# Attention, gated MLP and Fourier mixer in one kernel: MLP steps run closer behind the attention units, and weight conversion is tied to the exponentials

## The chip, the cores and the metric

One core of a Trainium2 chip runs the whole program in one launch. The metric is the device time in microseconds, the median of three runs.

## The reference

Three layers follow each other on four batches. Windowed attention with global tokens (32 global and 512 local tokens, 8 heads of 64) gives x of 544 x 512 a batch. A gated MLP takes h = max(x w_in, 0) with 1024 features, a three-tap convolution along the tokens, and returns (h * sigmoid(conv(h))) w_out. The mixer takes two Fourier transforms and keeps the real part, adds it, normalises over the features, and adds max(un w_ch1, 0) w_ch2 with 2048 hidden features:

```
a = softmax(scale * q k^T, window 32, global keys);  x = a v
h = max(x @ w_in, 0);  x = (h * sigmoid(conv3(h))) @ w_out
u = x + real(fft(fft(x, axis=1), axis=2))
out = u + max(norm(u) @ w_ch1, 0) @ w_ch2
```

The weights arrive as 64-bit numbers, which the kernel itself turns into 32-bit ones.

## The kernel before

**Order.** TensorE (PE) and the DMA queue of SyncE (SP) execute in the order in which the program is written. On ScalarE (ACT), VectorE (DVE) and GpSimd (POOL) a planner at build time chooses the order from the data dependences, its own estimate of the times and the priorities that the helpers carry; on the chip each of these engines then runs its list strictly in order. Every tile is guarded by semaphores.

**First stage: units.** A loop over i = 0 to 33 handles attention unit i (a half batch of one pair of heads; 32 of them, and two more rounds to drain). In unit i PE computes the scores of unit i (`s_mm`), the value products of unit i-2 (`pv_mm`), and the transposes of unit i-1 (`t_mm`). DVE adds the mask and finds the maxima (`s_max`, L311), ACT takes the four exponentials (`s_exp`, L323; the last one is kept in `last_exp`), POOL normalises (L334). Every second unit `pv_evac` copies two units' results into x, the high part by ACT (L389) and the rest by DVE (L390). For the global tokens `sg_piece` computes scores in units 8b+5 and 8b+7 with the banks s and t, emptied by DVE (L405); one unit later `pg_trans` transposes them, and two units later, in 8b+7 and 8b+9, `pg_pv` multiplies by v and has its bank copied into x by ACT (L449) and DVE (L450).

**MLP steps.** Between these, unit i runs two MLP steps, u = 2i-LU and u+1, of 64 (16 a batch: 8 feature blocks on the second half of the tokens, then 8 on the first half). Step u has `m_g1` (12 matmuls x by w_in into bank g1, emptied by ACT, L479), `m_conv` (ACT L489, DVE L490 and L491), `m_tanh` (ACT L497), `m_gate` (DVE L508, ACT L509, DVE L510), and three steps later `m_g2` (two halves of 6 matmuls g by w_out into banks a0 to a3). The steps that don't fit into the loop, from `ulast`+1 to 66, run after it. Up to unit SOLO-1 no `m_g2` runs, and attention may use the banks a0 to a3 and g1 as well.

**Weights.** Sixteen MLP weights are converted in units 0 to 8 (`make_w`): ACT (L167), POOL (L168), DVE or ACT for the tail (L172 or L170), DVE (L174, L175), then the split, ACT (L203) and DVE (L204). That block stands in `tc.issue_after(last_exp[0].ins)`: what it puts on ACT stands behind the last exponential of the unit in ACT's list. Twelve mixer weights go through the same conversion ahead of time: `keep_load` fetches the raw tile two units early (into r0 or r1), `keep_make` converts it (without that tie), `keep_store` writes it to DRAM as `kept`. `keep_at` gives them to units KEEP0, KEEP0+2, and so on.

**SP's list** in unit i is: `keep_load` for the tile of unit i+2, `load_qk(i+2)` (its buffer is free after `s_mm`, or `sg_piece`, of unit i-1), in odd units `load_v` (its buffer is free after `pv_mm`, in some after `pg_pv`), `keep_store` for the tile of unit i.

**After the loop** each remaining step takes two or three pieces of the Fourier transform (`fstep`; 49 pieces, of which the mixer's first nine steps take two each), with the banks s and t in turn. `ln` is the normalisation, `fetch_c(k)` loads kept or raw mixer weights. The mixer's 80 steps follow.

Of the kernel before, what the change touches and what calls it, by code (L numbers as in the profile page):

```python
# [26 lines left out]
KC = 608  # L27
NEG = -1.0e30
NF = 274
LU = 13  # L30
TOK = ((0, 290, 0, 292, 1, 1), (290, 254, 288, 256, 37, 39))
SOLO = 8
LAG_G2 = 3
KEEP0 = 10
KEPT = [0, 16, 1, 17, 2, 18, 3, 19, 4, 5, 6, 7]
TAIL = [x for m in range(8, 16) for x in (m, 16 + m)]
NT = 436
# [91 lines left out]
def fused_kernel(ctx: ExitStack, tc: tile.TileContext, d, out):  # L129
# [7 lines left out]
    def prio(c):  # L137
        def deco(f):
            def g(*a, **k):
                with pri(c):  # L140
                    return f(*a, **k)
            return g
        return deco
# [15 lines left out]
    def f32(ap):  # L159
        return ap.bitcast(F32)  # L160
# [40 lines left out]
    def put(pool, tag, val):  # L201
        t = pool.tile([128, 2, 512], F32R, tag=tag, name="w_" + tag)
        act.copy(t[:, 0], val)  # L203
        dve.tensor_sub(t[:, 1], val, f32(t[:, 0]))  # L204
        return t
# [12 lines left out]
    def bank(tag):  # L218
        return ps.tile([128, 512], F32, tag=tag, name="ps_" + tag)
# [25 lines left out]

    keep_at = {KEEP0 + 2 * k: x for k, x in enumerate(KEPT)}

    def keep_tile(i, lag):
        return keep_at.get(i - lag)
# [6 lines left out]
    @prio("keep")  # L256
    def keep_make(x):
        if x is not None:
            packed[x] = put(rb, "o", unpack(mp, w_raw.pop(x), gp, True))
# [22 lines left out]
    smalls, s_bank, last_exp = {}, {}, [None]  # L282
# [152 lines left out]
    @prio("glo")  # L435
    def pg_pv(g, tag):
        b, gg = divmod(g, 2)
        p, v = pg_t.pop(g), v_t[4 * b + 2 + gg]
        o = bank(tag)[:, 0:2 * SG].rearrange("p (c q) -> p c q", c=2)
        for c in range(2):  # L440
            for t in range(5):
                r = slice(0, 96 if t == 4 else 128)
                for h in range(2):
                    n = 2 * c + h
                    mm(o[64 * h:64 * h + 64, c], v[r, t, 64 * n:64 * n + 64], p[r, t, SG * n:SG * n + SG], t == 0, t == 4)
        xh, xl = get_xt(b)
        cs = slice(2 * gg, 2 * gg + 2)
        with pri("ev"):
            act.copy(xh[:, cs, 0:SG], o)  # L449
            dve.tensor_sub(xl[:, cs, 0:SG], o, f32(xh[:, cs, 0:SG]))  # L450
# [15 lines left out]
    @prio("mg1")  # L466
    def m_g1(u, tag):
        if not 0 <= u < NM:
            return
        b, half, m = u // 16, 1 - (u // 8) % 2, u % 8  # L470
        xh, xl = xt_t[b]
        _, _, t0, n, h0, _ = TOK[half]
        o = bank(tag)[:, 0:n]
        w = w_in[m]
        for c in range(4):
            f = slice(128 * c, 128 * c + 128)
            mm3(o, w[:, 0, f], w[:, 1, f], xh[:, c, t0:t0 + n], xl[:, c, t0:t0 + n], c == 0, c == 3)
        with pri("ev"):
            act.activation(hbuf[u % NHB][:, h0:h0 + n], o, AF.Relu, scale=0.5)  # L479
# [14 lines left out]
    @prio("me")  # L494
    def m_tanh(u):
        if 0 <= u < NM:
            act.activation(g_t[u], g_t[u], AF.Tanh, scale=0.5)  # L497
# [45 lines left out]
    with tc.manual_schedule(engines={mybir.EngineType.SP, mybir.EngineType.PE}):  # L543
        load_qk(0)
        sp.dma_start(mask[:, 2:4], d["mask"][:, 2:4])
        load_qk(1)
        sp.dma_start(ident, d["ident"])
        load_qk(2)
        for t in pbuf:
            dve.memset(t[:, :, 224:256], 0.0)  # L550
        for t in sg4s:
            dve.memset(t[:, KC:640], 0.0)
        for t in hbuf:
            dve.memset(t[:, 0:1], 0.0)
            dve.memset(t[:, 293:294], 0.0)
        dve.memset(f32(ones), 1.0 / 512.0)
        dve.memset(eps, 1e-6)

        NU = B * H
        glob = {8 * b + 5 + 2 * k: 2 * b + k for b in range(B) for k in range(2)}  # L560
        wq = [0] + [x for m in range(7) for x in (m + 1, 8 + m)] + [15]
        wsteps = [0, 1, 2, 4, 6, 8, 10, 12, 14, 16]
        fetched = 0
        craw = ap1.tile([128, 24, 2], I32, name="craw")
        cmag = ap1.tile([128, 24], F32, name="cmag")
        for i in range(NU + 2):
            r = i % 8
            live = i < NU
            early = i < SOLO
            us = [2 * i - LU, 2 * i - LU + 1]  # L570
            if live:
                first = s_mm(i, ("s", "t") if not early or i % 2 == 0 else ("a0", "a1"))
                if i == 0:
                    fetch_w(wq[0], first)
                    load_v(0)
                    sp.dma_start(mask[:, 0:2], d["mask"][:, 0:2])
                    fetched = 1
                while fetched < min(16, (2, 4, 7, 10, 13, 16)[min(i, 5)]):
                    fetch_w(wq[fetched])
                    fetched += 1  # L580
                if i == 1:
                    sp.dma_start(craw.rearrange("p a b -> p (a b)"), bits(d["conv_w"]))
                    gp.dma_start(gmask, d["gmask"])
                s_max(i)
            m_tanh(us[0] - 1)
            if 0 <= i - 2 < NU:
                pv_mm(i - 2, "pv" if not early or (i - 2) // 2 % 2 == 0 else "g1")
                if i % 2:
                    pv_evac((i - 2) // 2)
            if live:  # L590
                s_exp(i)
            m_g1(us[0], "g1")
            m_gate(us[0] - 1)
            m_conv(us[0])
            if live:
                s_norm(i)
            if 0 <= i - 1 < NU:
                t_mm(i - 1, ("s", "t") if not early or i % 2 == 0 else ("a2", "a3"))
                t_evac(i - 1)
            m_g2(us[0] - LAG_G2, 0)  # L600
            m_g2(us[0] - LAG_G2, 1)
            m_tanh(us[1] - 1)
            m_g1(us[1], "g1")
            if i > 5 and r in (6, 0):
                pg_trans(glob[i - 1], "s", "t")
            if i > 6 and r in (7, 1):
                pg_pv(glob[i - 2], "pv" if not early else "a3")
            if live and r in (5, 7):
                sg_piece(glob[i], 0, "s")
                sg_piece(glob[i], 1, "t")  # L610
                pg_soft(glob[i])
            m_gate(us[1] - 1)
            m_conv(us[1])
            m_g2(us[1] - LAG_G2, 0)
            m_g2(us[1] - LAG_G2, 1)
            keep_load(keep_tile(i, -2))
            if live and i > 0:
                load_qk(i + 2)
            if live and i % 2:
                load_v((i + 1) // 2)  # L620
            keep_make(keep_tile(i, 0))
            keep_store(keep_tile(i, 0))
            if i == 3:
                from_f64(craw, cmag)
                dve.tensor_scalar(convw2.rearrange("p a b -> p (a b)"), cmag, 2.0, None, op0=ALU.mult)
            if i < 9:
                with tc.issue_after(last_exp[0].ins):
                    for k in range(wsteps[i], wsteps[i + 1]):
                        make_w(wq[k])
        ulast = 2 * (NU + 1) - LU + 1  # L630
        right.close()
# [103 lines left out]
    @prio("cv")  # L735
    def fetch_c(i):
        pool, tag = c_slot(i)
        if i not in kept:
            w_raw[i] = fetch(pool, tag, c_src(i))
            return  # L740
        t = pool.tile([128, 2, 512], F32R, tag=tag, name="w_" + tag)
        sp.dma_start(f32(t), kept[i])
        (ch2 if i > 15 else ch1)[i % 16] = t
# [128 lines left out]
    def fstep(n=1):  # L872
        for _ in range(n):
            step(fq, "fft")
            for c, b in ((1, 1), (0, 2)):
                if b in u_d and c not in uc_t:
                    load_uc(c)
            if 0 in u_d and not lnq and not ln_t:
                lnq.append(ln(0))
                step(lnq)  # L880

    early = 7

    for u in range(ulast + 1, NM + LAG_G2):
        fstep()
        m_tanh(u - 1)
        m_g1(u, "g1")
        m_gate(u - 1)
        m_conv(u)
        if lnq and early:  # L890
            early -= 1
            step(lnq)
        fstep()
        m_g2(u - LAG_G2, 0)
        if u % 2 or u == ulast + 4:
            fstep()
        m_g2(u - LAG_G2, 1)
        if lnq and early:
            early -= 1
            step(lnq)  # L900
        k = u - (NM - 8)
        if 0 <= k < 8:
            fetch_c(k)
        if 0 <= k - 3 < 8:
            fetch_c(16 + k - 3)
    left.close()
# [74 lines left out]
```

## Time and profile before

| | us |
|---|---|
| median of three runs | 811.71 (811.49 to 812.03) |
| profiled execution, its own time | 815.52 |
| its span, first to last instruction | 813.7 |
| TensorE busy in it | 773.2 (95%) |
| VectorE, ScalarE, GpSimd busy | 480.0, 363.7, 156.1 |

The runs shown are 3.81 below the profiled execution. An engine's busy share is an average over stages with different limits, so the stages are read one by one below.

### The profile page before, as it was taken

How to read it: one execution, taken by the hardware profiler on the slowest of the kernel's cores; microseconds unless marked ns; L12 is line 12 of the kernel's file. 1: busy time of each engine (PE TensorE's matmuls, PEld its weight loads, DVE VectorE, ACT ScalarE, POOL GpSimd, SP SyncE). 2: the span in 40 equal slices, each digit the busy share in tenths (PEclk: the TensorE clock that was granted, in tenths of full speed). 3: DMA queues.
4: the chain of work that ended last, by engine and by line, in shares of the span. 5: the costliest groups of instructions: out<-in, count | busy, mean ns of one | idle time of the engine just before them, and what ended most of it. 6: DMA issues, size and time to landing. Idle time of an engine off the chain costs nothing.

```text
span 813.7 us, 13611 instructions
## 1 busy us (share of the span) xinstructions
PE 773.2 (95%) x5272; PEld 708.3 (87%) x5272; DVE 480.0 (59%) x1167; ACT 363.7 (45%) x884; POOL 156.1 (19%) x213
## 2 busy tenths in 40 slices
PE   6589999899999999999999999999999999999997
PEld 4378888798889888899988999998999999999997
DVE  6999886668676877679794587734421232223113
ACT  6788776567666666545344175412113112211110
POOL 5644521222222132000033012100013002200000
PEclk9779999899999999999999999999999999999999
DMA  8903603333333341226621290011020020001001
GB/s 314 389 34 106 213 28 124 131 132 108 124 129 117 128 131 54 61 78 236 202 104 49 76 379 16 1 41 48 23 67 1 1 88 1 1 1 44 1 1 44
DMA packets 36944, 77.80 MB, mean 96 GB/s; under 512 B 3768, under 2 KB 22072, under 8 KB 36880
## 3 DMA queue, kind: packets, MB, share of 16 engines
q1 hardware_dynamic: 36288, 74.52, 26.5%
q0 software_dynamic: 592, 2.42, 1.2%
q8 instruction: 41, 0.67, 0.3%
q14 instruction: 23, 0.19, 0.1%
HBM read 61.72 MB, written 15.20 MB: 95 GB/s over the span
## 4 chain that ended last, share of the span: by engine, by line
PE 74%; DVE 10%; DMA 9%; ACT 4%; SPq 1%; issue 1%; POOL 1%; DVEq 0%; POOLq 0%; ACTq 0%
PE ps_a L146 30%; PE ps_g L146 19%; PE ps_pv L146 14%; DMA raw_r<-in_ch_dram 7%; PE ps_s L146 5%; PE ps_t L146 4%; DVE mag L174 1%; DMA craw<-in_conv_w_dram 1%; DVE w_w L204 1%; DVE mag L175 1%; DMA uc<-u_d 1%; ACT mag L167 1%; DVE pb L311 1%; SPq L280 1%; ACT raw_r L170 1%
## 5 line engine op out<-in xcount | busy, mean ns | idle before, releaser
L146 PE MATMUL ps_g<-x,w_w 128*128 128x256 f32 (+1 forms) x768 | 113.0, 297 | 4.9 <-ACT h L479 4.9
L146 PE MATMUL ps_a<-g,w_w 128*128 128x254 f32 (+1 forms) x768 | 113.7, 297 | 0.2 <-DVE u L541 0.2
L146 PEld LDWEIGHTS ps_g<-x,w_w 128*128 128x128 f32 x768 | 102.0, 192 | 11.0 <-ACT h L479 6.0
L146 PEld LDWEIGHTS ps_a<-g,w_w 128*128 128x128 f32 x768 | 102.0, 192 | 4.5 <-issue 3.8
L334 POOL TENSOR_SCALAR pb<-pb,sm 128x224 f32<-128x224 f32 x128 | 75.6, 606 | 156.5 <-DVE sm L329 70.2
L146 PE MATMUL ps_a<-hd,w_w 128*128 128x436 f32 (+1 forms) x480 | 101.4, 360 | 0.0
L146 PEld LDWEIGHTS ps_a<-hd,w_w 128*128 128x128 f32 x480 | 90.1, 188 | 4.8
L825 DVE SCALAR_TENSOR_TENSOR hd<-ps_g,hd 128x436 fp32r<-128x436 f32 (+1 forms) x40 | 24.3, 608 | 89.2 <-ACT hd L824 89.2
L146 PE MATMUL ps_a<-hd,w_v 128*128 128x436 f32 (+1 forms) x360 | 76.2, 360 | 0.0
L825 DVE SCALAR_TENSOR_TENSOR hd<-ps_pv,hd 128x436 fp32r<-128x436 f32 (+1 forms) x40 | 24.2, 606 | 85.1 <-ACT hd L824 85.1
L824 ACT ACTIVATE hd<-ps_pv 128x436 fp32r<-128x436 f32 (+1 forms) x40 | 21.3, 532 | 114.9 <-PE ps_pv L146 114.9
L146 PEld LDWEIGHTS ps_a<-hd,w_v 128*128 128x128 f32 x360 | 67.6, 188 | 3.7
L824 ACT ACTIVATE hd<-ps_g 128x436 fp32r<-128x436 f32 (+1 forms) x40 | 21.3, 533 | 110.7 <-PE ps_g L146 110.4
L168 POOL TENSOR_SCALAR mag<-mag 128x512 f32<-128x512 f32 x48 | 36.8, 769 | 161.9 <-ACT mag L167 160.8
L323 ACT ACTIVATE pb<-pb,sm 128x224 f32<-128x224 f32 x128 | 60.4, 474 | 14.4 <-DVE sm L311 14.1
L490 DVE SCALAR_TENSOR_TENSOR y<-h,convw,y 128x254 f32<-128x254 f32 (+1 forms) x64 | 34.1, 533 | 33.9 <-ACT y L489 33.4
L146 PE MATMUL ps_g<-chl,w_w 128*128 128x436 f32 (+1 forms) x240 | 51.0, 361 | 0.0
L146 PE MATMUL ps_pv<-chl,w_v 128*128 128x436 f32 (+1 forms) x240 | 50.8, 360 | 0.0
L146 PE MATMUL ps_pv<-chl,w_w 128*128 128x436 f32 (+1 forms) x240 | 50.8, 360 | 0.0
L146 PE MATMUL ps_s<-qk 64*128 64x224 f32 (+1 forms) x144 | 38.6, 418 | 11.7 <-DMA qk<-in_qk_dram 6.9
L146 PEld LDWEIGHTS ps_pv<-chl,w_v 128*128 128x128 f32 x240 | 45.0, 188 | 2.5
L146 PEld LDWEIGHTS ps_g<-chl,w_w 128*128 128x128 f32 x240 | 44.8, 188 | 2.7 <-issue 0.3
(221 smaller groups left out, 1427.6 us busy)
## 6 DMA issues: line engine op xcount, KB each, us to landing
v<-in_v_dram SPq DMA_DIRECT2D x16, 640.0 KB, 4.4
qk<-in_qk_dram SPq DMA_DIRECT2D x16, 464.0 KB, 6.9
raw_r<-in_ch_dram SPq DMA_DIRECT2D x14, 512.0 KB, 6.3
raw_v<-in_ch_dram SPq DMA_DIRECT2D x13, 512.0 KB, 9.7
kept<-w_o SPq DMA_DIRECT2D x12, 512.0 KB, 7.7
w_w<-kept SPq DMA_DIRECT2D x12, 512.0 KB, 4.2
qk<-in_qk_dram SPq DMA_DIRECT2D x16, 304.0 KB, 6.4
u_d<-u SPq DMA_DIRECT2D x4, 1088.0 KB, 5.2
```

The lines of the kernel that those rows point to most:

```text
L146: return pe.matmul(o, a, b, start=start, stop=stop)
L167: act.activation(mag, f32(head), AF.Abs, scale=65536.0)
L168: (clamp or dve).tensor_scalar(mag, mag, TOP, 2.0, op0=ALU.min, op1=ALU.max)
L170: act.activation(tail, tail.bitcast(U32), AF.Copy, scale=0.999 * 2.0**-29, bias=-0.499)
L174: dve.scalar_tensor_tensor(val, val, 3, tail, op0=ALU.logical_shift_left, op1=ALU.bitwise_or)
L175: dve.scalar_tensor_tensor(val, head, -(2**31), val, op0=ALU.bitwise_and, op1=ALU.bitwise_or)
L204: dve.tensor_sub(t[:, 1], val, f32(t[:, 0]))
L323: last_exp[0] = act.activation(p, p, AF.Exp, bias=sm[:, k:k + 1], scale=-1.0, accum_out=sm[:, 4 + k:5 + k])
L334: gp.tensor_scalar(p, p, sm[:, k:k + 1], 1.0, op0=ALU.mult, op1=ALU.mult)
L490: dve.scalar_tensor_tensor(y, hb[:, cc - 1:cc - 1 + n], convw2[:, m, 0:1], y, op0=ALU.mult, op1=ALU.add)
L824: act.activation(hd[:, 0], o, AF.Relu)
L825: dve.scalar_tensor_tensor(hd[:, 1], o, 0.0, f32(hd[:, 0]), op0=ALU.max, op1=ALU.subtract)
```

## The change

`LU` goes from 13 to 11, so each unit runs MLP steps that are two further on, and two fewer steps are left behind the loop (10 instead of 12). `SOLO` goes from 8 to 7 with it, because the first `m_g2` now comes in unit 7. `KEEP0` goes from 10 to 11: the kept tiles go to odd units. `pg_pv` moves ahead of the unit's second `m_g1`, and always uses bank pv. `keep_make` is put behind the unit's last exponential on ACT. After the loop each step takes three pieces of the transform, and since the first such step is now 57, `fetch_c(0)` comes together with `fetch_c(1)`.

```diff
-LU = 13
+LU = 11
-SOLO = 8
+SOLO = 7
-KEEP0 = 10
+KEEP0 = 11
             m_tanh(us[1] - 1)
+            if i > 6 and r in (7, 1):
+                pg_pv(glob[i - 2], "pv")
             m_g1(us[1], "g1")
             if i > 5 and r in (6, 0):
                 pg_trans(glob[i - 1], "s", "t")
-            if i > 6 and r in (7, 1):
-                pg_pv(glob[i - 2], "pv" if not early else "a3")
...
-            keep_make(keep_tile(i, 0))
+            with tc.issue_after(last_exp[0].ins):
+                keep_make(keep_tile(i, 0))
             keep_store(keep_tile(i, 0))
...
         m_g2(u - LAG_G2, 0)
-        if u % 2 or u == ulast + 4:
-            fstep()
+        fstep()
         m_g2(u - LAG_G2, 1)
...
-        if 0 <= k < 8:
-            fetch_c(k)
+        for x in (0, 1) if k == 1 else (k,):
+            if 0 <= x < 8:
+                fetch_c(x)
```

## Rows read from the trace of the kernel before

**Rows 1.** The page: PE's busy time (parts 1 and 2).

```profile
PE 773.2 (95%) x5272; PEld 708.3 (87%) x5272; DVE 480.0 (59%) x1167; ACT 363.7 (45%) x884; POOL 156.1 (19%) x213
...
PEclk9779999899999999999999999999999999999999
```

**Rows 2.** Stages: length, then busy us of PE, PEld, DVE, ACT, POOL, clock, DMA.

```profile
29.86:83.15 53.29, 45.01 (x400) 36.72 (x399) 50.55 (x141) 42.56 (x111) 26.59 (x34) 0.88 0.37 131
...
120.00:337.30 217.30, 206.61 (x1901) 186.06 (x1899) 151.68 (x471) 139.71 (x396) 49.07 (x91) 0.98 0.34 110
337.30:405.70 68.40, 66.33 (x495) 61.70 (x492) 55.05 (x118) 32.43 (x74) 1.82 (x4) 1.00 0.51 164
```

**Rows 3.** PE's waits from 120 to 337.3: total us, times, longest.

```profile
PE ps_g L146 <- ACT h L479: 4.5, 3, 2.8
PE ps_t L429 <- ACT pt L353: 3.2, 3, 1.3
PE ps_s L344 <- DVE sm L311: 3.0, 2, 1.5
```

**Rows 4.** ACT's waits from 80 to 337: total us, times, longest.

```profile
ACT mag L167 <- DMA raw_r<-in_ch_dram: 18.8, 11, 3.0
```

**Rows 5.** The chain that ended last, at unit 14: start, us, what.

```profile
123.71 7.39 DMA raw_r<-in_ch_dram
...
131.13 0.68 ACT mag L167
```

**Rows 6.** Timeline: ACT's first exponential of unit 16 (start, us).

```profile
150.19 0.48 ACT L323 ACTIVATE pb<-pb,sm 128x224 f32<-128x224 f32 x1 [0.99 <-DVE sm L311]
```

**Rows 7.** Timeline: PE in unit 16, behind its longest wait.

```profile
156.29 2.93 PE L146 MATMUL ps_g<-x,w_w 128*128 128x256 f32 x12 [2.82 <-ACT h L479]
...
159.93 2.70 PE L146 MATMUL ps_a<-g,w_w 128*128 128x254 f32 x12
```

**Rows 8.** The stretch around it, columns as in rows 2.

```profile
155.40:162.30 6.90, 6.01 (x28) 6.02 (x29) 3.38 (x8) 3.85 (x11) 0.61 (x1) 0.51 0.03 9
```

**Rows 9.** PE's groups by shape, 100 to 400: busy us, mean ns, idle.

```profile
L146 PE MATMUL ps_a<-g,w_w 128*128 128x254 f32 x300 | 42.4, 291 | 0.0
L146 PE MATMUL ps_g<-x,w_w 128*128 128x256 f32 x288 | 40.7, 292 | 4.0 <-ACT h L479 4.0
```

**Rows 10.** DVE's groups by shape, 120 to 400: busy us, mean ns, idle.

```profile
L490 DVE SCALAR_TENSOR_TENSOR y<-h,convw,y 128x254 f32<-128x254 f32 x24 | 11.8, 490 | 16.0 <-ACT y L489 15.9
L508 DVE SCALAR_TENSOR_TENSOR y<-y,h 128x254 f32<-128x254 f32 x24 | 10.7, 446 | 6.5 <-ACT y L497 6.5
L510 DVE TENSOR_TENSOR g<-y,g 128x254 fp32r<-128x254 f32 x24 | 10.1, 419 | 3.9 <-ACT g L509 3.5
...
L204 DVE TENSOR_TENSOR w_o<-mag,w_o 128x512 fp32r<-128x512 f32 x9 | 6.2, 689 | 0.0
...
L174 DVE SCALAR_TENSOR_TENSOR mag<-mag,raw_r 128x512 int32<-128x512 int32 x9 | 6.2, 684 | 0.0
```

**Rows 11.** Timeline: DVE empties the bank g1 in unit 5.

```profile
38.46 0.68 DVE L390 TENSOR_TENSOR x<-ps_g,x 128x512 fp32r<-128x512 f32 x1
```

**Rows 12.** Timeline: PE from the global scores of unit 5 to unit 6.

```profile
36.38 0.68 PE L146 MATMUL ps_t<-qk 128*64 128x304 f32 x4
41.39 1.11 PE L146 MATMUL ps_s<-qk 64*128 64x224 f32 x2 [4.33 <-DVE smg L405]
```

**Rows 13.** Timeline: `pg_pv` and its two copies in unit 17.

```profile
169.87 1.36 PE L146 MATMUL ps_pv<-pgt,v 128*64 128x32 f32 x40
...
171.27 0.21 ACT L449 CAST x<-ps_pv 128x64 fp32r<-128x64 f32 x1
...
172.06 0.22 DVE L450 TENSOR_TENSOR x<-ps_pv,x 128x64 fp32r<-128x64 f32 x1
```

**Rows 14.** Timeline: a POOL addition and a DVE conversion together, after 404.

```profile
406.67 2.10 POOL L773 TENSOR_TENSOR cf<-uc 128x872 f32<-128x872 f32 x1 [1.23 <-DMA uc<-u_d]
...
407.47 1.85 DVE L174 SCALAR_TENSOR_TENSOR mag<-mag,raw_w 128x512 int32<-128x512 int32 x1
```

## The prediction

> **What bounds the kernel now.** I read the page first, then the busy time by stage, the waits of PE and of ACT, the chain that ended last, and the timeline around each wait. TensorE is busy for 773.2 us of 813.7 [rows 1], so what can be won without taking work away is its idle time, about 40 us, and the stretches at half clock that the PEclk line shows near the start and once near 160 us.
>
> The stages say where that idle time lies [rows 2]. From unit 5 to unit 10 (29.86 to 83.15) PE is busy for 45.01 of 53.29 us, so 8.3 are idle, while DVE is busy for 50.55, or 95%: here DVE is the bound, because it converts the sixteen MLP weights beside its ordinary work. From 120 to 337.3 PE is busy for 206.61 of 217.30, 10.7 idle, with DVE at 70%: PE is the bound and loses time to single waits. In the stage behind the loop PE is busy for 66.33 of 68.40 and DVE for 55.05: only 2.1 are idle.
>
> The 10.7 us are eight waits of three kinds [rows 3]. Six of them (4.5 and 3.2) are for a bank that ACT empties. ACT itself stood still then: eleven of the twelve kept tiles made it wait for their raw data, 18.8 us together [rows 4]. The chain shows how: a raw tile takes 7.39 us from issue to landing and ACT's first conversion starts 0.03 us after that, at 131.13 [rows 5]. This tile belongs to unit 16 in the program, whose exponentials start at 150.19 [rows 6]. So the planner had put the conversion some two units ahead of its place in the program and believed the data to be there; ACT's list is strict, and all emptying of banks queued behind an absent tile.
>
> **The tie (kept tiles behind their unit's exponentials).** It moves ACT's first conversion of that tile from 131 to 150 or later, 19 us behind the time at which its data landed [rows 5, 6]. The load keeps its place two units ahead, and one of 7.39 us fits easily. So the waits for raw data should go altogether. Of PE's waits the six for ACT fall away: -7.7. The third kind, two waits for DVE's maxima (3.0 together), sit in units where DVE also has the MLP banks to empty; that work stays, so I take -1.2, with 0 and -3.0 as bounds. One wait of 2.82 us was followed by half clock: from 155.4 to 162.3 the granted clock is 0.51, so nearly all at 1.2 GHz [rows 7, 8]. Two groups of 12 matmuls took 2.93 and 2.70 us there, against 1.70 each elsewhere (40.7 us by 288 matmuls, 42.4 by 300, times 12) [rows 7, 9]: 1.23 + 1.00 = 2.2 to be had back. Bounds: 0, if another idle stretch brings the low clock, and -2.2.
>
> What is late next? A tile's conversion doesn't vanish. DVE does three operations of 0.68 to 0.69 for it (L175 is like L174), 2.06 us [rows 10], now in the second half of an odd unit or in the next. The odd units also have the copies of `pv_evac` and the global scores. DVE's 70% over this stage is 7.1 us in a unit of 10.1 (21.5 units in 217.3); moving the tiles from even to odd units makes the odd ones heavier by about 1.0 than the mean, so 8.1, and with the odd units' own work nearer 9. That fits, with short queues: +1.5 for eleven tiles, between 0 and the price of the slow rival below. `keep_store` stands in SP's list behind this conversion and holds back `load_qk` of the next unit, but that load is wanted two units later, some 20 us, so I price it at nothing; without this cover it would be a load's 7 us. `keep_load` now stands in front of the odd unit's `load_v` instead of behind the previous one, so it can only start earlier.
>
> **Two steps earlier (LU, SOLO).** By the start of unit 10 PE has done two more MLP steps, that is four groups of 12 matmuls at 1.70: 6.8 us of work that no longer stands behind the loop [rows 9]. DVE has to do their share too: L490 and its twin L491 0.49 each, L508 0.45, L510 0.42, so 1.85 a step, 3.7 us, in the one stage in which DVE is the bound [rows 2, 10]. If unit 10 starts later by DVE's 3.7 less some 0.4 of its 2.7 us of idle time, the net is -6.8 + 3.3 = -3.5. Best case: the 8.3 idle us of PE take all of it, -6.8. Worst case 0: step 0 now falls into unit 5, where bank g1 holds value products that DVE empties only at 38.46 to 39.14 [rows 11]; its 12 matmuls run then, perhaps at the low clock (2.93 [rows 7]), and only behind them the global scores, which before ended at 37.06 [rows 12]. Unit 6 waited until 41.39 because DVE reached those scores late [rows 12]; another 2 to 3 us on top of the 3.7 would use up the gain.
>
> **The global product ahead of `m_g1`.** With LU = 11 step 16b+8 is the second step of unit 8b+9, and it reads the tokens that `pg_pv` of that unit has just produced. So it must follow, and now it waits for the two copies. In unit 17 the matmuls end at 171.23, ACT copies from 171.27, and DVE is done at 172.28, since another operation stood ahead: 1.05 us [rows 13]. Six of the 12 matmuls, 0.85 us, read features that were ready long before. So a batch pays at least 0.2, and at most 1.05 + 0.68 - 0.85 = 0.9 if DVE has a conversion (0.68, rows 10) in front. Middle: 0.6 a batch, +2.3 for four; bounds +0.8 and +3.6. Queued behind the waiting `m_g1` are `pg_trans` or the scores, and both `m_g2`; ACT and DVE don't depend on them at once. The other close pair, `pv_evac` ahead of step 16b in unit 8b+5, has a first step, transposes and two `m_g2` halves between (over 4 us), so it costs nothing outside unit 5.
>
> **Behind the loop.** Thirty pieces of the transform in ten steps replace 31 in twelve. PE does 6.8 less there, DVE 3.7 less of 55.05. DVE's share goes from 80% to (55.05 - 3.7) / (68.40 - 6.8) = 83%, but the normalisation and the denser pieces meet in its second half. I take +1.5 for waits on the banks s and t, with -1 and +4 as bounds. `fetch_c(0)` one step later has the rest of the loop as cover.
>
> **Sum.** -7.7 - 1.2 - 2.2 + 1.5 - 3.5 + 2.3 + 1.5 = -9.3. Against the span of 813.7 that gives 804.4; the runs lie 3.81 below the profiled execution's 815.52, as 811.71 shows, and so I forecast 802.4 for them.
>
> **The rivals.** (a) The front gives nothing and the new waits are at their upper bounds: -7.7 - 1.2 - 2.2 + 1.5 + 0 + 3.6 + 4 = -2.0, so 809.7; with half of that ill luck -5, so 806.7. For it speaks DVE's 95% in the front [rows 2], against it that two kept tiles (4.1 us of DVE) leave the units 9 to 11. (b) More comes: the front takes all 6.8, all DVE waits go, no new ones come: -7.7 - 3.0 - 2.2 - 6.8 + 0.8 = -18.9, so 793. (c) Slower: the tied tiles crowd DVE in the odd units. POOL's four normalisations follow the exponentials, and the tile's POOL step stands behind them; if DVE's list meets the tile before POOL is done, DVE stops, the maxima of the next unit are late, and PE waits as it did in the third kind, 1.5 [rows 3]. For eleven tiles that is 16.5 in place of the 1.5 of my sum: -9.3 + 15.0 = +5.7, so 817.4. It decides from 0.95 us a tile on ((9.3 + 1.5 - 0.4) / 11). Against it: the planner sees POOL's queue, unlike a late DMA. A second part of this mechanism is visible: beside a POOL addition that ran from 406.67 to 408.77, DVE's L174 took 1.85 in place of 0.68 [rows 10, 14].
>
> The Trainium skill, SBUF — State Buffer, "SBUF: two separate sides", has a rule behind that row: a VectorE operation with two SBUF inputs and a GpSimd operation that reads SBUF hold one pair of ports exclusively, and the loser waits for the whole instruction. The row just named agrees with it. By that rule each tied tile's L174, L175 and L204 may meet POOL's normalisations; it would make rival (c) likelier than the idle share of DVE alone suggests, and its time would be that of (c).
>
> (d) No change: the planner gains by moving the tiles as much as it loses elsewhere, within 0.2% (1.6 us, about what a measurement of this kernel can tell from no change).
>
> **How the numbers follow.** My forecast, -5 to -14 with DVE and the new waits near their middles: 62%. (b) 8%, (a) 15%, (d) 5%, (c) 10%. Faster by over 0.2%: 62 + 8 + 15 = 85%; within: 5%; slower: 10%. The range reaches down to 794, almost all of (b), and up to 810, the end of (a); left out are (d), (c) and a sliver of (b), somewhat under 2 in 10.
>
> **What would show it.** In the trace after: ACT's row of waits for raw data (18.8) gone or under 2; PE's waits for ACT's h and pt from 120 to 337 gone; no half clock near 160; four short waits of the first matmuls on new global tokens in units 9, 17, 25 and 33, under 1 us each; unit 10 starting at 84 to 87; the stage behind the loop 5 to 7 us shorter. Wrong would make it: PE's waits for DVE's maxima in most odd units, a front that ends over 6 us later, or waits for the banks s and t in the transform.

## The result, and the profile after

The changed kernel takes **803.37 us** (median of 4 runs, 803.11 to 805.17), the kernel before 811.87 beside it (811.49 to 814.04): a ratio of 0.9895, 95% interval 0.9872 to 0.9917. So it is about 1% faster, 8.5 us, where the prediction had 802.4. The profiled execution took 803.62, its span is 801.6.

The page of after, part 1 and the clock line of part 2, answers to [rows 1]:

```profile
PE 769.5 (96%) x5272; PEld 705.8 (88%) x5272; DVE 481.1 (60%) x1167; ACT 364.4 (45%) x884; POOL 157.4 (20%) x213
...
PEclk9789999999999999999999999999999999999999
```

The work is the same (5272 matmuls), and the slice near 160 us that showed a lower clock is at full speed. The rows of the prediction have these answers in the trace after.

PE's waits from unit 10 to the end of the loop, for [rows 3] (each row: total us, times, longest):

```profile
PE ps_g L146 <- DVE x L450: 1.5, 2, 0.8
```

The three kinds of [rows 3] are all gone, and one new kind has come, the wait for `pg_pv`'s copies (a third one of 0.82 us lies just ahead of this stretch). ACT's waits from 80 to 330 us, for [rows 4]:

```profile
ACT y L497 <- DVE y L491: 33.2, 36, 1.3
ACT h L479 <- PE ps_g L146: 9.7, 15, 1.2
ACT g L509 <- DVE y L508: 9.7, 13, 1.3
```

The row of 18.8 us for raw data has no successor at any place of the list. Why not is in ACT's timeline in unit 17 (start, us, what), for [rows 5, 6]:

```profile
163.08 0.48 ACT L323 ACTIVATE pb<-pb,sm 128x224 f32<-128x224 f32 x1
163.46 0.19 ACT L323 ACTIVATION_READ_ACCUMULATOR pb<-pb,sm 128x1 f32 x1
163.56 0.66 ACT L167 ACTIVATE mag<-raw_r 128x512 f32<-128x512 f32 x1
164.12 0.68 ACT L170 ACTIVATE raw_r<-raw_r 128x512 int32<-128x512 uint32 x1
164.68 0.38 ACT L479 ACTIVATE h<-ps_g 128x256 f32<-128x256 f32 x1
```

The conversion (L167) stands right behind the unit's fourth exponential, as the tie demands, and starts without a wait. The bank that PE needs (L479) is emptied 1.1 us later, not behind an absent tile.

One step of the prediction already looks wrong here. PE's timeline in unit 5, and its longest wait in unit 6 (the bracket is the idle time before and what ended it), for [rows 12]:

```profile
39.11 2.93 PE L146 MATMUL ps_g<-x,w_w 128*128 128x256 f32 x12 [3.31 <-DVE x L390]
41.97 1.28 PE L146 MATMUL ps_s<-qk 128*64 128x304 f32 x4
...
51.68 1.68 PE L146 MATMUL ps_g<-x,w_w 128*128 128x256 f32 x12 [2.03 <-ACT h L479]
```

Step 0 waits for bank g1, its 12 matmuls take 2.93 us (the granted clock from 39.11 to 41.9 is 0.50), and the global scores follow it at 41.97, where before they had ended at 37.06 [rows 12]. Unit 10 starts at 89.7 instead of 83.15.

### The profile page after: what moved, and what is told of

Its sections match the earlier page's. It is cut to its first block, busy times and chain, and to the rows that moved or that the text cites. A ratio compares the mean times of both kernels' runs of the same rounds, so it can differ in the third digit from the quotient of the medians.

```text
span 801.6 us, 13594 instructions
## 1 busy us (share of the span) xinstructions
PE 769.5 (96%) x5272; PEld 705.8 (88%) x5272; DVE 481.1 (60%) x1167; ACT 364.4 (45%) x884; POOL 157.4 (20%) x213
## 4 chain that ended last, share of the span: by engine, by line
PE 79%; DVE 10%; DMA 5%; ACT 4%; issue 1%; POOL 1%; SPq 0%; POOLq 0%; DVEq 0%; ACTq 0%
PE ps_a L146 32%; PE ps_g L146 22%; PE ps_pv L146 14%; PE ps_s L146 5%; PE ps_t L146 3%; DMA raw_w<-in_w_in_dram 2%; DMA uc<-u_d 1%; ACT pb L323 1%; DVE mag L174 1%; DVE mag L175 1%; DVE pb L311 1%; DVE y L491 1%; DMA u_d<-u 1%; DVE uc L857 1%; DVE y L490 1%
## 5 line engine op out<-in xcount | busy, mean ns | idle before, releaser
L334 POOL TENSOR_SCALAR pb<-pb,sm 128x224 f32<-128x224 f32 x128 | 77.0, 620 | 92.7 <-DVE sm L329 33.4
L168 POOL TENSOR_SCALAR mag<-mag 128x512 f32<-128x512 f32 x48 | 38.7, 808 | 151.7 <-ACT mag L167 150.5
L146 PEld LDWEIGHTS ps_pv<-chl,w_w 128*128 128x128 f32 x240 | 44.9, 188 | 2.5
```

The source lines that it names most:

```text
L146: return pe.matmul(o, a, b, start=start, stop=stop)
L168: (clamp or dve).tensor_scalar(mag, mag, TOP, 2.0, op0=ALU.min, op1=ALU.max)
L334: gp.tensor_scalar(p, p, sm[:, k:k + 1], 1.0, op0=ALU.mult, op1=ALU.mult)
```

## The experiments

All times below are medians. Kernels that ran together on one chip share runs of the kernel before (medians 812.53 for 1, 2, 3 and 6; 812.47 for 4, 5, 8 and 9; 813.81 for 7, 10 and 11; 812.05 for 12), and the ratio is to those.

**1. The kernel before, once more.** No edit.

> The kernel before, unchanged, profiled once more. The first profile of it lay 3.7 us above the median of its runs (815.52 against 811.87). If that profile held a stretch that ordinary executions lack, this span is near 809.7 to 810.5 and the half clock near 160 us or one of the eight waits of PE is smaller. If profiling itself costs that much with this kernel, the span is again near 813.7 with the same waits.

Measured: 812.12, ratio 0.9989 (0.9966 to 1.0012), span 810.0. The first profile of before was 3.7 longer in its span. The difference has a place, unit 16: it lasts 15.06 us in the first profile (147.50 to 162.56) and 10.72 in this one. The matmuls that follow the wait of 2.82 us in [rows 7] have this row here:

```profile
155.29 1.70 PE L146 MATMUL ps_g<-x,w_w 128*128 128x256 f32 x12 [1.15 <-ACT h L479]
```

A wait of 1.15, and the 12 matmuls at their 1.70 rather than 2.93: no half clock behind it. So this profile is the one that belongs to the median, and the comparisons by stage below use it.

**2. The tie alone.** The kernel before with

```diff
-            keep_make(keep_tile(i, 0))
+            with tc.issue_after(last_exp[0].ins):
+                keep_make(keep_tile(i, 0))
```

> Before, with only the tie of the kept tiles added (still LU 13, even units). Theory: PE lost its time in the unit loop to ACT waiting for raw tiles, so the tie alone brings most of the gain: ACT's row of waits for raw data (18.8 us) vanishes, PE's waits for ACT's h and pt vanish, 7 to 10 us faster (802 to 805). Rival: the lag did it, and the tie only moves the waits to DVE: 0 to 3 us faster (809 to 812).

**3. The rest alone.** The changed kernel without that tie, with `KEEP0 = 10`.

> After, without the tie and with the tiles in even units as before (LU 11, pg_pv ahead, three pieces a step). Theory: the lag gives back in a later unit 10 (+6.5 us measured) what it saves behind the loop (-5.0), so alone it is worth between -1 and +3 us (811 to 815), and ACT's waits for raw tiles are there again, 15 to 20 us in total. Rival: the lag is worth 5 us or more by itself (807 or less).

Measured: the tie alone **796.25** (ratio 0.9792, 0.9765 to 0.9819), everything but the tie **817.22** (ratio 1.0051, 1.0028 to 1.0073). Both lie outside their first theory's range: the tie gave 16.3 us instead of 7 to 10, and the rest lost 4.7 instead of at most 2.5 (812.53 to 815). The tie by itself is 7 us better than the whole change, and the rest is a loss. The stages, with their borders taken from PE's timeline (the first scores of units 10 and 31, the mixer's first matmuls); below, the first of them is called the front, and the lag is the value of `LU`:

| us | before again | whole change | tie alone | rest alone |
|---|---|---|---|---|
| start to unit 10 | 83.1 | 89.7 | 83.8 | 90.0 |
| unit 10 to unit 31 | 222.7 | 210.8 | 207.8 | 224.9 |
| unit 31 to the mixer | 96.3 | 90.7 | 95.4 | 91.9 |
| mixer | 407.9 | 410.4 | 407.9 | 408.9 |
| span | 810.0 | 801.6 | 794.9 | 815.7 |

The second line is in the main the tie's (the rest adds 2.2 to 3.0 to it); the other lines change with the rest. The busy times of that second line (length, then PE, PEld, DVE, ACT, POOL, clock, DMA), before again:

```profile
83.10:305.80 222.70, 211.80 (x1907) 190.89 (x1906) 162.87 (x508) 149.49 (x430) 59.23 (x105) 1.00 0.38 124
```

and the tie alone, followed by its stage behind unit 31 and its mixer:

```profile
83.80:291.60 207.80, 207.80 (x1908) 190.46 (x1907) 163.77 (x507) 148.26 (x430) 56.00 (x103) 1.00 0.36 128
291.60:387.04 95.44, 93.29 (x789) 86.43 (x789) 74.75 (x173) 50.73 (x119) 6.81 (x12) 1.00 0.43 140
387.04:794.90 407.86, 401.03 (x2063) 378.46 (x2061) 169.84 (x259) 101.36 (x168) 48.94 (x34) 1.00 0.14 50
```

PE's 10.9 idle us become none at all: the list of its waits in this stretch is empty. The waits that went, in the second profile of before:

```profile
PE ps_s L344 <- DVE sm L311: 4.2, 3, 1.7
PE ps_t L429 <- ACT pt L353: 3.6, 3, 1.8
PE ps_g L146 <- ACT h L479: 2.5, 3, 1.1
PE ps_t L344 <- DVE sm L311: 0.6, 1, 0.6
```

Those on DVE's maxima (4.2 and 0.6) went with the ones on ACT. How an absent tile reaches them is in the timelines of before again in unit 12, ACT's first, then DVE's and PE's:

```profile
101.47 0.66 ACT L167 ACTIVATE mag<-raw_r 128x512 f32<-128x512 f32 x1 [1.28 <-DMA raw_r<-in_ch_dram]
...
102.89 0.45 ACT L509 CAST g<-y 128x290 fp32r<-128x290 f32 x1
...
103.37 0.46 DVE L510 TENSOR_TENSOR g<-y,g 128x290 fp32r<-128x290 f32 x1 [2.61 <-ACT g L509]
...
105.78 0.38 DVE L311 CUSTOM_DVE_ANT_0 pb<-ps_s,mask 128x224 f32<-128x224 f32 x1
...
107.06 0.30 PE L344 MATMUL ps_s<-ident,pb 128*128 128x128 f32 x1 [1.16 <-DVE sm L311]
```

ACT waits for the tile, DVE stands idle for 2.61 us behind ACT, its maxima come late, and PE waits. The waits of units 20 and 28 (1.41 and 1.67) have the same chain, with 1.94 and 1.97 for the tile and DVE idle for 2.16 and 2.19 behind ACT's L497. With the tie alone, unit 12 has no wait for a tile and none of PE's, and its maxima start 2.05 us behind its first scores (103.92 and 101.87) instead of 3.75 (105.78 and 102.03).

The other 4.0 of the 14.9 us are in the stretch's busy time (211.80 against 207.80), though the mean of each large group of matmuls stays within 2 ns. They belong to the stalls too. Eight of the 21 units wait for nothing before again, and they last as long with the tie alone (to 0.01 us, unit 11 for instance 9.14 and 9.13). The ten units with a wait are longer by 0.13 to 0.38 beyond their idle time, 2.5 together, and three without a listed wait by 0.25 to 0.65, 1.5 together. In units 15 and 23 the scores in bank t start 0.5 us behind those in bank s (135.89 and 136.42 in unit 15), where otherwise both start within 0.01. So the idle time of PE's rows understates a stall.

**4. Odd units alone.** The tie alone, with `KEEP0 = 11`.

> The kernel before with the tie, and the kept tiles at odd units (from unit 11) as the whole change has them; lag 13 and the pieces of before. Theory: the tie does the work, because it puts the conversions where their data has long landed; in even or odd units they cost the scalar engine the same 2.1 us per unit, so 795 to 798 us, within 0.25% of the tie at even units (796.25), and no wait of TensorE over 1 us between units 10 and 31. Rival: odd units are crowded, because the mixer's partial products (pg_pv) of every eighth odd unit and the conversions share VectorE and ScalarE there; then a wait on the bank g2 or s of about 0.3 us in each of the eleven odd units shows, and the time is 799 to 801 us: that would put about 3 of the 7 us between the tie alone and the whole change on the parity.

Measured: 797.88, ratio 0.9824 (0.9797 to 0.9850), which overlaps the tie alone; the profiled span is 794.1 against 794.9, and the list of PE's waits from unit 10 to unit 31 is empty here too. Odd or even makes no difference that these runs can tell.

**5. Earlier loads in place of the tie.** The kernel before with

```diff
-            keep_load(keep_tile(i, -2))
+            keep_load(keep_tile(i, -3))
```

> The kernel before, without the tie, with each kept tile loaded three units before its conversion instead of two. Theory A (the data is late): the ScalarE waits on the raw tiles end because the transfer is issued 8 us earlier and lands ahead of the conversion; the time falls as with the tie, to 796 to 800 us. Theory B (the conversion stands too early in the order): the conversion is placed ahead of the unit's exponentials as soon as the planner's own estimate of the transfer's end allows it, so an earlier load moves the conversion earlier too, the ScalarE waits stay at about 0.5 to 1.8 us a tile, and the time stays at 810 to 814 us. In A the waits of ScalarE on the raw tiles are under 0.2 us at all twelve tiles; in B they stand at most of them.

Measured: 813.61, ratio 1.0013 (0.9985 to 1.0040); the profiled execution is one of the slower ones (817.23). Theory B's time holds, its list of waits only in part. ACT's waits from unit 10 to unit 31:

```profile
ACT w_o L203 <- DMA kept<-w_o: 14.5, 8, 4.3
...
ACT mag L167 <- DMA raw_r<-in_ch_dram: 5.2, 5, 1.7
```

and its timeline at one tile:

```profile
152.22 0.62 ACT L203 CAST w_o<-mag 128x512 fp32r<-128x512 f32 x1 [1.50 <-DMA kept<-w_o]
...
154.89 0.66 ACT L167 ACTIVATE mag<-raw_r 128x512 f32<-128x512 f32 x1 [1.55 <-DMA raw_r<-in_ch_dram]
```

The tile of the second row belongs to unit 20 in the program and is converted while PE is in unit 16, four units ahead of its place; in [rows 5, 6] it was two. With the load earlier, the planner moved the conversion earlier too. What it then waits for is partly the data again, mostly the store that still empties its output tile. ACT stands still for 19.7 us as before (17.6 in the second profile of before, 18.8 in [rows 4]). So it isn't late data as such; it is a place in ACT's strict list at which something the planner misjudged is still under way. The tie changes the place.

**6. `pg_pv` earlier.** The changed kernel with `pg_pv` between the transposes and the unit's first `m_g2`.

> After, with pg_pv one place further ahead, between the transposes and the two m_g2 halves, so that about 1.6 us of matmuls lie between it and the m_g1 that reads its tokens. Theory: the three waits for x L450 (2.3 us together) vanish; pg_pv itself may wait some 0.3 us more for bank pv, emptied by pv_evac 2.1 to 2.5 us after its matmuls while pg_pv comes 2.6 us after them. 1 to 2.5 us faster than after (801 to 802.5). Rival: pg_pv meets pv_evac and waits as long as it saves: no change.

Measured: 804.33, ratio 0.9890 (0.9865 to 0.9915), no gain. The waits on L450 are gone and the units 10 to 31 take 209.2 instead of 210.8, but unit 10 starts at 94.5 instead of 89.7, where these are PE's waits from 30 us on:

```profile
PE ps_g L146 <- DVE x L390: 3.3, 1, 3.3
PE ps_pv L146 <- DVE x L390: 3.1, 2, 1.8
```

`pg_pv` itself now comes too early for its bank. That isn't all of the 4.8 us: PE's idle time from 30 us to unit 10 is 11.6 (9.3 in the changed kernel) and its busy time 52.9 (50.4), at a clock of 0.89 (0.94). The profiled execution is the slowest of the six (806.44), so part of this may be its own.

**7. `pg_pv`'s new place alone.** The tie alone (lag 13), with `pg_pv` ahead of the second `m_g1` and always in bank pv.

> The tie alone (lag 13, 796.25 us), with pg_pv moved ahead of the unit's second m_g1 and always in the bank pv, as the whole change has it. Theory: the wait of TensorE on VectorE's subtraction at line 450 is the price of the new place and comes back here without the shorter lag: three waits of 0.7 to 0.9 us near units 10, 18 and 26, about 2.3 us, and 798 to 800 us. Rival: the wait belongs to the place together with the lag of 11, because the lag decides which MLP step stands at units 10, 18 and 26; then no wait on line 450 above 0.2 us and 795.5 to 797 us.

Measured: **795.24**, ratio 0.9784 (0.9753 to 0.9815): the rival. No wait on L450, and none at all from unit 10 to unit 31. It is the fastest median of the study, but its interval overlaps that of the tie alone. With lag 13 the `m_g1` behind `pg_pv` doesn't read the new tokens; with 11 it does. DVE's timeline in unit 17 of the changed kernel shows what makes it wait there:

```profile
166.51 0.68 DVE L174 SCALAR_TENSOR_TENSOR mag<-mag,raw_r 128x512 int32<-128x512 int32 x1
167.11 0.58 DVE L491 SCALAR_TENSOR_TENSOR y<-h,convw,y 128x254 f32<-128x254 f32 x1
167.62 0.68 DVE L175 SCALAR_TENSOR_TENSOR mag<-raw_r,mag 128x512 int32<-128x512 int32 x1
168.22 0.21 DVE L450 TENSOR_TENSOR x<-ps_pv,x 128x64 fp32r<-128x64 f32 x1
```

A kept tile's conversion (L174, L175) stands in front of the copy. The rest alone, which has lag 11 and the tiles in even units, shows no such wait in units 17 and 25. In unit 9, ahead of the first kept tile, both kernels have one (0.82 and 0.38), and there the conversion of an MLP weight (L175, L204) stands in front. So the wait seems to need the lag and a conversion in that unit; the changed kernel with even tiles wasn't run.

**8 to 10. The lag with the tie.** The tie alone with `LU = 12, SOLO = 7`, with `LU = 14` and with `LU = 15` (two or three pieces a step, as before).

> The tie alone, with a lag of 12 steps instead of 13 (one step moved from behind the loop into the front). Theory: the front is bound by VectorE there, so the moved step adds its own time to it: unit 10 starts about 3 us later than with the tie alone (83.8, so 86.5 to 87.5), the part behind the loop is about 2.5 us shorter, and the time is 796 to 799 us. Rival: the idle time of TensorE in the front takes the first moved step, and only the second, with the solo stage that ends a unit earlier, cost something: unit 10 at 84 to 85, and 793 to 795 us, the best of all.

> The tie alone, with a lag of 14 steps instead of 13 (one step moved from the front to behind the loop). Theory (the front gives a step's own time for each one, the part behind the loop takes most of it): unit 10 starts 2 to 3 us earlier than 83.8, the part behind the loop is 2.5 to 2.9 us longer, the time is 795.5 to 798 us, so the lag is worth nothing either way around 13. Rival: each step taken out of the front gives 3 us and the mixer gets some back as well, as the step from 11 to 13 did with 7 us in all: 792 to 794 us.

> The tie alone, with a lag of 15 steps instead of 13 (two steps moved out of the front to behind the loop). Lags 12 and 14 each came out about 2 us above lag 13 and showed two or three waits of 0.9 to 1.2 us on VectorE's line 541, where two token halves meet within one unit; an odd lag has no such meeting. Theory: without these waits the remaining terms nearly cancel: unit 10 at about 80 (two steps fewer at 2 us each), the part behind the loop up by 4 to 5 us, the mixer down by 2 to 4 us because more transform pieces run ahead of it; 794 to 797 us, that is within 0.3% of lag 13. Rival: the front has no more to give once its steps are gone and the part behind the loop takes them at 2.5 us each, 799 to 801 us.

| lag | median, ratio | unit 10 at | PE busy and idle from 30 us to there | 10 to 31 | 31 to mixer | mixer |
|---|---|---|---|---|---|---|
| 11 (whole change) | 803.37, 0.9895 | 89.7 | 50.4, 9.3 | 210.8 | 90.7 | 410.4 |
| 12 | 797.94, 0.9822 (0.9802 to 0.9841) | 85.7 | 47.8, 7.9 | 211.0 | 88.7 | 410.8 |
| 13 (tie alone) | 796.25, 0.9792 | 83.8 | 45.7, 8.1 | 207.8 | 95.4 | 407.9 |
| 14 | 798.99, 0.9840 (0.9820 to 0.9860) | 81.8 | 44.0, 7.8 | 210.6 | 99.3 | 405.6 |
| 15 | 808.38, 0.9940 (0.9915 to 0.9966) | 78.7 | 37.9, 10.8 | 208.8 | 105.1 | 411.3 |

Lag 12 comes out inside its first theory's range (797.94 for 796 to 799) and lag 14 one above it (798.99 for 795.5 to 798); both rivals with a better optimum fall. By their intervals lag 12 and lag 13 can't be told apart. The parts were forecast less well: with lag 12 the stretch from unit 31 to the mixer is 6.7 shorter where 2.5 was expected, and the mixer 2.9 longer. One reason is in the program: the lags also differ in the transform pieces behind the loop (27, 31, 32 and 36 for lags 12 to 15, 30 in the whole change), and the mixer takes what is left. So the last two columns belong together; they add up to 501.1, 499.5, 503.3, 504.9 and 516.4. Lag 15 misses both of its ranges (the profiled execution, 806.46, lies 1.9 below its median). From unit 31 to the mixer it takes 9.6 more than lag 13, where 4 to 5 were expected, and in its mixer stand two waits on the last transform's data that lag 13 lacks:

```profile
PE ps_t L146 <- DVE fl L662: 3.4, 1, 3.4
PE ps_t L146 <- DVE fl L666: 3.0, 1, 3.0
```

The even lags have a wait of their own between units 10 and 31, here lag 14:

```profile
PE ps_a L146 <- DVE u L541: 2.6, 3, 0.9
```

Where the second token half of a batch gives its banks to the next half within one unit, PE must wait for DVE to empty them; lag 15 lacks this row, as expected. The fourth column is the point for the prediction. From lag 14 to 11 PE's busy time in the front grows by 1.7 to 2.6 us with each step, and its idle time stays at 8 to 9 us (10.8 with lag 15). Part of that busy time is at the lower clock, less so the more steps there are: the granted clock of the stretch is 0.80, 0.84, 0.88 and 0.94 from lag 14 to lag 11.

The row of lag 11 is the whole change, which differs in the pieces, the odd units and the place of `pg_pv` too. Experiments 4 and 7 show that the odd units and that place cost nothing clear of noise at lag 13. The tie with `LU = 11` and nothing else wasn't run, so how the 5.4 us between lag 12 and the whole change divide stays open; 4.0 of them are in the front (85.7 to 89.7).

**11. Less DVE work in the front.** The changed kernel, with the tail shift (L172) on ACT for all sixteen MLP weights.

```diff
-unpack(mp, w_raw.pop(i), gp, i % 2 == 0)
+unpack(mp, w_raw.pop(i), gp, True)
```

> The whole change, with the shift of the weights' lower words (line 172) on ScalarE for all sixteen weight tiles instead of eight: VectorE loses eight instructions, 4.5 us in all, 2.3 us of them after 30 us; ScalarE gains eight at 0.66 us. Theory: VectorE, busy 93% from 30 us to unit 10, sets the front's length; so unit 10 starts 1.5 to 4 us earlier than 89.7, and the time is 799.5 to 802 us. Rival: chains of short dependent instructions set it (transposes, exponentials, evictions); then unit 10 moves by less than 1 us or comes later, as ScalarE's copies queue behind the added work, and the time is 803 to 806 us.

Measured: 802.78, ratio 0.9870 (0.9838 to 0.9901); unit 10 at 89.8. The front of the changed kernel, and then the same stretch here:

```profile
30.00:89.70 59.70, 50.38 (x449) 41.13 (x448) 55.53 (x151) 44.27 (x118) 25.16 (x36) 0.94 0.37 133
```

```profile
30.00:89.80 59.80, 51.03 (x452) 41.76 (x451) 52.79 (x147) 47.68 (x127) 25.70 (x37) 0.93 0.37 136
```

DVE has 2.7 us less to do and the stretch is as long as it was. In this execution unit 4's scores, which wait for their input in both (2.95 us here, 4.32 in the other), started 1.2 us later (25.60 against 24.39), and unit 5 with them (31.2 against 30.0); counted from unit 5, the front is 1.1 shorter. So DVE's load is worth some 1.1 of 2.7 there, by one execution of each; it is not what sets the length alone. The time lies between the two ranges and is, by its interval, that of the changed kernel.

**12. The bank of step 0.** The changed kernel, with the value products that units 4 and 5 compute in bank pv (and those of units 2 and 3 in g1).

```diff
-pv_mm(i - 2, "pv" if not early or (i - 2) // 2 % 2 == 0 else "g1")
+pv_mm(i - 2, "g1" if i < 4 else "pv")
```

> The whole change, with the value products of units 4 and 5 in the bank pv instead of g1, so that the first matmuls of MLP step 0 in unit 5 find their bank empty instead of waiting 3.31 us for VectorE's subtraction at line 390. Theory: in the front TensorE loses a nearly fixed 8 to 9 us to such chains whatever stands in it (8.1 idle from 30 us to unit 10 with lag 13, 9.3 with lag 11), and the two moved steps cost their own matmul time; the wait then turns up at the next link, unit 6's scores as in the kernel before or step 1's first matmuls: unit 10 comes less than 1.5 us earlier than 89.7, the time is 801.5 to 804 us. Rival: this one wait is what spoils the front, since step 0 came to stand in unit 5 ahead of the global scores; then unit 10 starts 3 us or more earlier, at 86.7 or before, and the time is 799 to 801 us.

Measured: 803.91, ratio 0.9911 (0.9888 to 0.9935); unit 10 at 88.5, 1.2 earlier. PE's waits from 30 us on:

```profile
PE ps_g L146 <- ACT h L479: 2.0, 1, 2.0
PE ps_g L146 <- DVE x L390: 1.5, 1, 1.5
PE ps_s L146 <- ACT pgt L431: 1.0, 1, 1.0
PE ps_a L344 <- POOL pb L334: 0.9, 2, 0.5
PE ps_g L146 <- DVE x L450: 0.8, 1, 0.8
PE ps_g L146 <- ACT x L389: 0.7, 1, 0.7
```

The wait of 3.31 became 1.5 on the same subtraction for the next step and 0.7 on ACT's copy. The theory holds: of the one wait removed most turns up at the next link, and PE's idle time from 30 us to unit 10 falls only from 9.3 to 8.4.

## Why the prediction came out nearly right

The time was right to 1.0 us, by two errors of nearly 7 us that cancel; that is luck. The steps of the sum fall into the tie (-7.7 - 1.2 - 2.2 + 1.5 = -9.6) and the rest (-3.5 + 2.3 + 1.5 = +0.3). Measured apart, the tie is worth -16.3 (812.53 to 796.25) and the rest costs +7.1 on top of it (to 803.37), or +4.7 without it (812.53 to 817.22).

- **The tie, -7.7 for ACT: right in its mechanism, too small with its neighbours.** The row of 18.8 vanished and the six waits with it. The term that failed is "-1.2" for DVE's maxima, because "that work stays": all waits on L311 went, 4.8 us in the second profile of before. DVE's work did stay, 163.8 us between units 10 and 31 against 162.9, so it wasn't the work that made PE wait; DVE had been held up behind the blocked ACT, as the timelines of unit 12 show (experiment 2). The sum also priced each wait at its idle time, and with what lies around it the waits cost another 4.0 us.
- **-2.2 for half clock: counted, but not to be had from the median.** The second profile of before has a wait of 1.15 and no slow matmuls at that place. The sum charged the change with a stall of one execution and then also took off the 3.81 by which the runs lie below that execution. By spans the change gave -12.1 (813.7 to 801.6) against -9.3; by medians -8.5.
- **Kept work at its new place, +1.5: nothing by itself.** The tie in even and in odd units leaves PE without a wait from unit 10 to unit 31, and DVE's L174, L175 and L204 take 0.68, 0.68 and 0.69 us in this stretch of the changed kernel, as in [rows 10]. So rival (c) fell. Nor does the tile's POOL step always stand behind the normalisations, as (c) had it: in seven of ten units it ran ahead of them (in unit 17, L168 at 164.30 and L334 from 165.01). The Trainium skill (SBUF — State Buffer, "SBUF: two separate sides") says that a VectorE operation with two SBUF inputs and a GpSimd operation that reads SBUF exclude each other for the whole instruction. The trace agrees, but here GpSimd is the one that loses, where it was VectorE in [rows 14]: ten of these thirty operations run beside POOL's normalisations and still take 0.68, while a unit's four normalisations take 3.38 us beside L174 and L175 (from 104.65) and 1.75 beside neither (from 123.02). PE waits for none of them in this stretch.
- **The front, +3.3 for unit 10: the step that failed most.** It is +6.6 against the second profile of before, and +5.9 between the tie alone and the whole change. The sum held that "unit 10 starts later by DVE's 3.7 less some 0.4 of its 2.7 us of idle time"; PE's idle time was to take the rest. It took nothing: from 8.1 with the tie alone it went to 9.3, and PE's busy time rose by 4.7, less than the 6.8 of the two steps, while the stretch's clock rose from 0.84 to 0.94. (One wait of `pg_pv`, 0.82, lies in unit 9 and is part of the 5.9.) Against the 4.7 to 5.6 won behind the loop that leaves a loss of about 1, where -3.5 + 1.5 = -2.0 was forecast. The prediction's worst case, with step 0 in unit 5 ahead of the global scores, is what the trace shows, and the sign that it set for being wrong (a front over 6 us later) came true. Which resource sets the front's length stays open: neither DVE's load (experiment 11) nor the one bank (12) does so alone. Rival (a) was right in this point, and its time (806.7 to 809.7) was missed because the tie gave more.
- **`pg_pv`, +2.3: right in its sum.** Three waits of 0.82, 0.76 and 0.74 are 2.3 us; predicted were four of 0.6. The three lie near the prediction's upper bound of 0.9, which it gave for a conversion in front of the copy; in unit 33, where no conversion stands in front, no wait is listed.
- **Behind the loop, -6.8 + 1.5 = -5.3: right in its sum.** From unit 31 to the mixer it is 5.6 shorter (96.3 to 90.7). PE's busy time fell by 5.8 there and its idle time stayed (2.5 before again, 2.6 here). One wait of 1.85 us is followed by half clock, which is part of the busy time:

```profile
382.00 0.35 PE L146 MATMUL ps_s<-co,fl 1*92 1x258 f32 x1 [1.85 <-DVE fl L666]
382.19 0.28 PE L146 MATMUL ps_s<-co,fh 1*92 1x258 f32 x1
382.40 1.79 PE L146 MATMUL ps_a<-g,w_w 128*128 128x290 f32 x6
```

```profile
382.40:385.80 3.40, 3.40 (x16) 3.40 (x16) 0.94 (x3) 0.67 (x2) 0.00 (x0) 0.51 0.60 225
```

- **The mixer, not in the sum: +2.5.** The prediction said that thirty pieces replace 31 and did not ask where the thirty-first goes. It goes into the mixer, whose stage has 9 more matmuls:

```profile
300.50:391.17 90.67, 88.08 (x732) 81.02 (x732) 71.59 (x164) 48.31 (x113) 6.72 (x12) 0.98 0.48 151
391.17:801.60 410.43, 402.72 (x2072) 379.05 (x2070) 168.60 (x261) 101.19 (x167) 49.66 (x35) 1.00 0.14 49
```

PE is busy 1.7 us longer there than with the tie alone (402.72 against 401.03) and idle 0.9 longer. Among the changed kernel's variants the stage took 408.9 to 412.7, so the size is loose; the piece put back into the loop wasn't tried.

## What to carry to other kernels

A planner at build time places optional work by its own guess of when a transfer ends, and a strict list then makes every instruction behind it pay. Tie such work to an event that surely lies behind its data (here 2% of the time for one line). An earlier load alone, here, only let the planner move the work along.

Idle time of PE in a stage that is full of short dependences need not be room for more matmuls: from lag 14 to lag 11 a moved step of 3.4 us of matmuls made the front longer by 1.9 to 4.0, and the idle time stayed at 7.8 to 9.3. And run the parts of a change apart: a total near the forecast hid a gain of 16 us and a loss of 7.

## What the runs showed that was not expected

Two profiles of one kernel differed by 3.7 us in span, and one unit by 4.3. The wait in it was 2.82 us in one and 1.15 in the other, and only the longer wait was followed by a granted clock of 0.51 [rows 8]. So a stall read from a single profile may be that execution's own.

Idle time ahead of a stretch went with a lower clock elsewhere too: a wait of 1.85 us in the changed kernel was followed by 3.4 us at 0.51, while the waits of 0.74 and 0.76 on L450 were not: the 12 matmuls behind the one in unit 17 took 1.58 us, and the clock from unit 10 to unit 31 is 1.00 to two digits. But the length of the wait doesn't settle it. In unit 6 the changed kernel waits 2.03 us for L479, and the 12 matmuls behind it take 1.68 at a clock of 1.00 (shown with the result); in experiment 6 the same wait is as long, and they run at 0.50:

```profile
51.35 2.93 PE L146 MATMUL ps_g<-x,w_w 128*128 128x256 f32 x12 [2.03 <-ACT h L479]
```
